# Talking-heads attention with a squared-ReLU FFN: output products that wait for their own quarter of w_out, output evictions ranked last

## The chip, the cores and the metric

The kernel runs on one core of a Trainium2 chip. The metric is the device time of one execution in microseconds, the median of the runs taken. The chip's engines are named as in the profile: PE (TensorE, the matrix engine), DVE (VectorE), ACT (ScalarE), POOL (GpSimd) and SP (SyncE, which issues transfers here). PEld is TensorE's loading of weights, which runs beside its products.

## The reference

Attention over 8 batches, 12 heads, 448 positions and 64 values per head, in which the heads are mixed before and after the softmax, then an FFN with a squared ReLU on all 3584 tokens.

```python
scores = scale * np.matmul(q, k.transpose(0, 1, 3, 2))
scores = np.einsum('bhij,hg->bgij', scores, w_pre)
attn = softmax(scores)                       # over the last axis
attn = np.einsum('bhij,hg->bgij', attn, w_post)
x = np.matmul(attn, v)                       # as (3584, 768)
h = np.maximum(x @ w_in, 0.0)                # w_in (768, 2048)
out = h * h @ w_out                          # w_out (2048, 768)
```

## The kernel before

**The attention.** A batch is cut into 45 chunks of about 10 query rows times 12 heads, 120 of the 128 partitions. For a chunk, TensorE mixes the scores of the heads (lines 901, 907 and, for two chunks at once, 847), VectorE takes the minimum (line 912; the signs are turned), ScalarE the exponential with its sums (line 915), VectorE the reciprocal of the sums (line 922, once for two chunks), GpSimd scales the weights of the second mixing with it (`wq`, line 925), and TensorE forms the mixed attention transposed, four products per chunk (line 932). VectorE or ScalarE copies it to `atb` (the helper `copy`, lines 534 and 536). Scores come from line 741 into `snat` and are laid out anew into the tiles `sch` by transfers that SP issues (`relayout`, line 772). The product with v is line 978. Lines 741 (from batch 1 and for three of four blocks), 847 and 978 run on 64-wide parts of the array, the others on all of it.

**The FFN.** Tokens go in units of 128 or 256 columns of `xt` (`unit`, line 1020). A unit has hidden blocks (line 1037, six products for each 128 of the 2048 hidden values), their ReLU (lines 1051 and 1055) and square (line 1058), and then output blocks: for each 128 tokens two halves of the 768 output columns (0 to 383 and 384 to 767), 16 products each over the hidden values, entered in pairs (`OSTEP = 2`, line 1076). The last 128 tokens have three blocks instead of two. That makes 57 output blocks. Each is copied to `osb` (line 1091) and stored from there (line 1100).

**w_out.** It is loaded in four transfers (`load_w2`, line 1184), each 8 of the 16 hidden groups times one half of the columns: quarters 0 and 1 are the first and second 1024 hidden values of columns 0 to 383, quarters 2 and 3 those of the other columns. They are entered at the chunks of `W2_AT` (14, 17, 20 and 23 of batch 0). The first pair of every output block waits for all four, so the later pairs' own wait adds nothing.

**What sets the order.** All instructions are entered into a planner (`Planner`, line 129) with their dependencies, an estimated duration and a priority, the smaller the earlier; for attention it is the chunk's number with a small offset. The planner goes through time and gives each engine the ready instruction with the smallest priority; that order is then written into the engines' queues, which run it strictly in order. Where an operation has two possible engines, the first that is free takes it. FFN products have priorities of a million and more, so they fill TensorE when attention has nothing ready. The copies of output blocks have priority 0, and so come ahead of nearly all attention work. `AHEAD` is by how many chunks the transfers of `relayout` and the scores rank ahead of the chunk that needs them. An FFN block holds one of eight PSUM banks until it is copied out, and the FFN may hold two at a time (`MOST`). Where TensorE would have nothing up to 130 us of planned time, the planner puts in a matmul on zeros (`stand`, line 1301, the tile `still`), if the array has lately been little used.

Of the kernel before, what the change touches and what calls it, by code (L numbers as in the profile page):

```python
# [19 lines left out]
ACT = mybir.ActivationFunctionType  # L20
# [20 lines left out]
PIECE = NPAIR // 2  # L41
NE = 6
NSCH = 14
AHEAD = 7.0
FIFO = 50
IDLE_NS, IDLE_COLS, IDLE_FROM, IDLE_END, IDLE_LOW = 112, 256, 1300, 130000, 0.62
SPELL, PHASE, DROP, RISE = 3413, 1700, 0.4, 0.8
# [9 lines left out]
OSTEP = 2  # L57
# [28 lines left out]
SOON = 0  # L86
# [42 lines left out]
class Planner:  # L129
# [8 lines left out]
    def add(self, eng, ns, pri, fn, deps=(), lat=60, bank=None, frees=None, mode=0):  # L138
        op = Op(eng if isinstance(eng, dict) else {eng: ns}, lat, pri, fn, list(deps), bank, frees, mode)
        self.ops.append(op)  # L140
        return op
# [199 lines left out]
def kernel(  # L341
# [190 lines left out]
    def copy(eng, out_, in_):  # L532
        if eng == "DVE":
            nc.vector.tensor_copy(out=out_, in_=in_)  # L534
        else:
            nc.scalar.copy(out=out_, in_=in_)  # L536
# [4 lines left out]
    add = pl.add  # L541
    FILL = 1e6
    slots = {}
# [12 lines left out]
    def keep(key, fn):  # L556
        def go(*got):
            for key_, slot in zip(key if isinstance(key, list) else [key], got):
                slots[key_] = slot
            fn(*got)  # L560
        return go
# [10 lines left out]
    m_op, max_op, exp_op, rc_op, wq_op, at_op, ac_op = {}, {}, {}, {}, {}, {}, {}  # L572
    av_op, xc_op = {}, {}
    h_op, sq_op, o_op, st_op = {}, {}, {}, {}
# [137 lines left out]
    def place_of(b, c):  # L712
        return b * NCHUNK + (ORDER0.index(c) if b == 0 else c)
# [4 lines left out]
    direct, prep_op = [], []  # L718

    def is_direct(b, c):  # L720
        return b == 0 and C0[1] <= c <= C0[2]
# [5 lines left out]
    def score(b, r, group):  # L727
# [50 lines left out]
    def relayout(b, c):  # L778
# [6 lines left out]
        deps = list(scopy[b, r]) + (list(scopy[b, r - 1]) if r == 1 and cc == 0 else [])  # L785
        pri = n - AHEAD
        if r == 2 and cc == 0:
# [15 lines left out]
        else:  # L803
            o = cc - 1
            if b >= PAIR_FROM:
                pri = n - o % (2 * PAIRS) + 0.1 * (o % (2 * PAIRS)) - AHEAD
            o, step = (2 * CI * (o // 2) + o % 2, 2) if b >= PAIR_FROM else (o, CPR)
# [207 lines left out]
    def units_of(pair):  # L1015
        return UNITS if pair else UNITS0
# [3 lines left out]
    def unit(pair, ui):  # L1020
        a, z = units_of(pair)[ui]
        w = z - a
        nf = 512 // w
        ix = len(units)
        units.append((pair, ui))
        h2_ = h2[ix % 2]
        fill = FILL + 100 * ix
        xdeps = [op for t0, t1, op in xc_op[pair] if t0 < z and t1 > a]
        old_o = o_op.get(ix - 2, [])
        h_op[pair, a], sq_op[ix], o_op[ix] = [], [], []  # L1030
        prev = None
        for f0 in range(0, FT, nf):
            key = ("f", ix, "h", f0)
            for j in range(nf):
                def mms(slot, f0=f0, j=j):
                    for c2 in range(NPAIR):
                        nc.tensor.matmul(  # L1037
                            slot[:, j * w:(j + 1) * w], lhsT=w1[c2][:, (f0 + j) * 128:(f0 + j + 1) * 128],
                            rhs=xt[:, c2, a:z], start=(c2 == 0), stop=(c2 == NPAIR - 1),
                        )  # L1040
                if j == 0:
                    prev = add("PE", w * 2.55, fill + f0, keep(key, mms), xdeps + w1_in + [prev], lat=0, bank=key)
                else:
                    prev = add("PE", w * 2.55, 0, lambda key=key, mms=mms: mms(slots[key]), [prev], lat=0)
                h_op[pair, a].append(prev)
            end = add("WAIT%s" % str(key), 0, 0, lambda: None, [prev], lat=200)
            gi = len(hr_log)

            def relu(eng, key=key, gi=gi):
                if eng == "DVE":  # L1050
                    nc.vector.tensor_scalar(  # L1051
                        out=hr[gi % 2][:, :], in0=slots[key][:, :], scalar1=0.0, scalar2=0.0, op0=ALU.max, op1=ALU.add,
                    )
                else:
                    nc.scalar.activation(out=hr[gi % 2][:, :], in_=slots[key][:, :], func=ACT.Relu)

            def square(gi=gi, f0=f0):
                nc.gpsimd.tensor_tensor(  # L1058
                    out=h2_[:, f0:f0 + nf, 0:w],
                    in0=hr[gi % 2][:, :].rearrange("p (f c) -> p f c", f=nf),  # L1060
                    in1=hr[gi % 2][:, :].rearrange("p (f c) -> p f c", f=nf), op=ALU.mult,
                )

            rl = add({"ACT": 500, "DVE": 590}, 0, 0, relu, [end, hr_log[gi - 2] if gi >= 2 else None], lat=100, frees=key)
            sq = add("POOL", 1020, FILL, square, [rl] + old_o, lat=70)
            hr_log.append(sq)
            sq_op[ix].append(sq)
        for mt in range(w // 128):
            whole = not (z == W2B and mt == 1 and pair == B // 2 - 1)
            cuts = [0, 384, DMODEL] if whole else [0, 384, 640, DMODEL]  # L1070
            for nt, (c0, c1) in enumerate(zip(cuts, cuts[1:])):
                key = ("f", ix, "o", mt, nt)
                for f0 in range(0, FT, OSTEP):
                    def mms(slot, f0=f0, mt=mt, c0=c0, c1=c1):
                        for ft in range(f0, f0 + OSTEP):
                            nc.tensor.matmul(  # L1076
                                slot[:, 0:c1 - c0], lhsT=h2_[:, ft, mt * 128:(mt + 1) * 128],
                                rhs=w2[:, ft, c0:c1],
                                start=(ft == 0), stop=(ft == FT - 1),
                            )  # L1080
                    if f0 == 0:
                        prev = add("PE", (12 + (c1 - c0) * 5 // 3) * OSTEP / 4, fill + 20 + 4 * mt + 2 * nt, keep(key, mms),
                                   [prev] + sq_op[ix][0:max(1, OSTEP // nf)] + w2_in[0:1 if ix < SOON else 4], lat=0, bank=key)
                    else:
                        prev = add("PE", (12 + (c1 - c0) * 5 // 3) * OSTEP / 4, FILL, lambda key=key, mms=mms: mms(slots[key]), [prev, w2_in[f0 // 4]] + sq_op[ix][0:(f0 + OSTEP + nf - 1) // nf], lat=0)
                    o_op[ix].append(prev)
                end = add("WAIT%s" % str(key), 0, 0, lambda: None, [prev], lat=200)
                si = ix_store[0]

                def evac(eng, key=key, si=si, c0=c0, c1=c1):  # L1090
                    copy(eng, osb[si % 2][:, c0:c1], slots[key][:, 0:c1 - c0])

                ev = add({"DVE": 80 + (c1 - c0) * 25 // 24, "ACT": 165 + (c1 - c0) * 5 // 7}, 0, 0, evac, [end, st_op.get(si - 2)] + ([m_op[n_] for n_ in direct] if si < 2 else []), lat=100, frees=key)
                evs = evs + [ev] if nt == 1 and whole else [ev]
                if nt == 1 or not whole:
                    done = []
                    for rows, dst, o in pieces(pair, a + mt * 128, None if whole else (c0, c1)):
                        side_ = not whole and rows <= CI
                        def store(dst=dst, o=o, rows=rows, si=si, e0=0 if whole else c0, e1=DMODEL if whole else c1, eng=nc.scalar if side_ else nc.gpsimd if whole else nc.sync):
                            eng.dma_start(out=dst, in_=osb[si % 2][o:o + rows, e0:e1])  # L1100
                        done.append(add("ACT" if side_ else "POOL" if whole else "SP", 510 if rows <= CI else 830 if whole else 930, FILL, store, evs))
                    for op in done:
                        op.store = whole
                    st_op[si] = pl.moved("LOAD" if whole else "DMA", 64, 16, 16, 0, done, 700)
            if whole:
                ix_store[0] += 1
# [70 lines left out]
    w2_in = [add("W2", 0, 0, lambda: None, lat=0) for i in range(4)]  # L1177
# [32 lines left out]
    def first_batch():  # L1210
# [35 lines left out]
        for gs in ONE:  # L1246
            av(0, 1, gs, P_ROWS, XB)
        unit(0, 2)

    def next_batch(b):  # L1250
# [91 lines left out]
```

## Time and profile before

| | |
|---|---|
| time before, median of 3 runs | 571.62 us (571.61 to 571.78) |
| profiled execution | 571.9 us, span 570.1 us |
| granted TensorE clock | 0.999 |
| PE, DVE, ACT, POOL busy | 561.1, 500.8, 446.4, 363.0 us |
| instructions at lines 1037, 1076, 932, 1301 on PE | 1632, 912, 1440, 50 |

The span goes from the first to the last instruction; the time of an execution also holds what lies around it. Busy time is the time in which at least one instruction of the engine ran. In the views, a row `start, duration, engine, line, operation, out<-in, xN` merges N instructions that follow each other, and `[idle before <-releaser]` tells how long the engine stood before it and what ended that. Products overlap in the engine, so the duration of a merged row reaches beyond the next row's start; differences of starts tell how long the engine was taken.

### The profile page before, as it was taken

Reading aid. Unit: us, or ns where it says so; the run is one execution under the profiler, and the core shown is the slowest. Engines: PE = TensorE matmul, PEld = TensorE weight load, DVE = VectorE, ACT = ScalarE, POOL = GpSimd, SP = SyncE. Lnnn points to the kernel's source line nnn. Section 1 sums busy time; section 2 is a strip of 40 time slices with the busy share of each in tenths; the row PEclk is TensorE's granted clock in tenths of the full one; section 3 lists DMA queues with packets and bytes.
Section 4 is the critical chain, followed back from the end, with each engine's and each line's share of the span. In section 5 each row is a group of like instructions: output and inputs, shape, how many; then the busy total and the mean of one; then the engine's idle time right before and its main releaser. Section 6 shows DMA issues by size and latency. Waiting matters only on the chain.

```text
span 570.1 us, 17924 instructions
## 1 busy us (share of the span) xinstructions
PE 561.1 (98%) x6340; PEld 398.5 (70%) x6340; DVE 500.8 (88%) x1109; ACT 446.4 (78%) x1186; POOL 363.0 (64%) x677
## 2 busy tenths in 40 slices
PE   8999999999999999999999999999999999999997
PEld 5667765776677767677667677767667677767785
DVE  7999999999999899989888899998899998998542
ACT  5789988788788888888887888987888878888400
POOL 8667346776677448857578456957569554736451
PEclk9999999999999999999999999999999999999999
DMA  9999859974896739964797739975399656542011
GB/s 136 210 177 223 162 122 184 189 146 111 154 208 120 166 101 178 189 149 113 125 213 122 166 101 160 195 163 138 65 208 171 143 139 113 119 103 79 1 56 55
DMA packets 129949, 80.85 MB, mean 142 GB/s; under 512 B 59274, under 2 KB 126588, under 8 KB 129860
## 3 DMA queue, kind: packets, MB, share of 16 engines
q1 hardware_dynamic: 80756, 46.29, 37.0%
q0 software_dynamic: 49104, 33.43, 36.2%
q8 instruction: 49, 0.80, 0.6%
q14 instruction: 40, 0.33, 0.2%
HBM read 45.61 MB, written 11.01 MB: 99 GB/s over the span
## 4 chain that ended last, share of the span: by engine, by line
PE 90%; DVE 6%; POOL 1%; DMA 1%; issue 1%; ACT 0%; DVEq 0%; POOLq 0%; ACTq 0%
PE bank L1076 27%; PE bank L1037 25%; PE bank L932 13%; PE bank L741 7%; PE bank L978 7%; PE bank L847 5%; PE bank L901 3%; PE bank L907 2%; DVE mn L912 1%; DVE snat L534 1%; DMA sch<-snat 1%; DVE atb L534 1%; PE bank L1301 1%; DVE hr L1051 1%; DVE osb L890 1%
## 5 line engine op out<-in xcount | busy, mean ns | idle before, releaser
L915 ACT ACTIVATE es<-bank,mn 124x448 bf16<-124x448 f32 (+1 forms) x360 | 228.1, 642 | 42.9 <-DVE mn L912 35.8
L912 DVE TENSOR_REDUCE mn<-bank 124x1 f32<-124x448 f32 (+1 forms) x360 | 209.4, 613 | 3.9 <-PE bank L847 3.4
L1076 PE MATMUL bank<-w,h 128*128 128x384 bf16 (+2 forms) x912 | 177.3, 323 | 0.2
L1037 PE MATMUL bank<-xt,w 128*128 128x256 bf16 (+1 forms) x1632 | 164.1, 254 | 0.6 <-DVE hr L1051 0.3
L1037 PEld LDWEIGHTS <-w 128*128 128x128 bf16 x1632 | 132.8, 98 | 25.8 <-issue 12.2
L925 POOL TENSOR_SCALAR wq<-wback_two,rc 124x120 bf16<-124x120 f32 x252 | 88.8, 362 | 86.3 <-DVE rc L922 60.2
L1058 POOL TENSOR_TENSOR h<-hr 128x512 bf16<-128x512 f32 x112 | 115.7, 1037 | 33.1 <-DVE hr L1051 15.1
L932 PEld LDWEIGHTS <-es 124*112 124x112 bf16 (+2 forms) x1440 | 108.0, 129 | 32.5 <-issue 8.8
L534 DVE CAST atb<-bank 112x480 bf16<-112x480 f32 (+3 forms) x196 | 119.1, 617 | 10.6 <-PE bank L932 9.6
L932 PE MATMUL bank<-wq,es 124*112 124x120 bf16 (+2 forms) x1440 | 120.2, 217 | 2.0 <-POOL wq L925 1.5
L1076 PEld LDWEIGHTS <-h 128*128 128x128 bf16 x912 | 80.2, 98 | 55.0 <-issue 16.1
L536 ACT CAST atb<-bank 112x480 bf16<-112x480 f32 (+3 forms) x187 | 98.2, 539 | 16.1 <-PE bank L932 14.5
L536 ACT CAST snat<-bank 128x448 bf16<-128x448 f32 x168 | 84.6, 543 | 11.4 <-PE bank L741 10.6
L534 DVE CAST snat<-bank 128x448 bf16<-128x448 f32 x150 | 89.8, 614 | 0.8 <-PE bank L741 0.3
L1051 DVE TENSOR_SCALAR hr<-bank 128x512 f32<-128x512 f32 x82 | 56.6, 690 | 21.1 <-PE bank L1037 15.7
L915 ACT ACTIVATION_READ_ACCUMULATOR es<-bank,mn 124x1 f32 (+1 forms) x360 | 75.0, 208 | 0.0
L925 POOL TENSOR_SCALAR wq<-wback,rc 124x120 bf16<-124x120 f32 (+1 forms) x94 | 33.6, 365 | 39.3 <-DVE rc L922 26.1
L741 PE MATMUL bank<-kt,qz 64*64 64x448 bf16 (+1 forms) x528 | 44.6, 361 | 0.1
L847 PE MATMUL bank<-sch,wmix 64*64 64x448 bf16 x504 | 42.7, 363 | 0.0
L978 PE MATMUL bank<-atb,vs 112*64 112x192 bf16 (+3 forms) x864 | 40.4, 250 | 0.2 <-DVE atb L534 0.2
L978 PEld LDWEIGHTS <-vs 112*64 112x64 bf16 x864 | 36.5, 110 | 5.0 <-issue 4.5
L1100 POOL DMA_DIRECT2D out_dram<-osb x33 | 19.9, 604 | 29.9 <-DVE osb L534 16.4
(80 smaller groups left out, 397.7 us busy)
## 6 DMA issues: line engine op xcount, KB each, us to landing
sch<-snat SPq DMA_DIRECT2D x318, 105.0 KB
out_dram<-osb POOLq DMA_DIRECT2D x21, 384.0 KB, 3.8
vs<-in_v_dram POOLq DMA_DIRECT2D x16, 336.0 KB, 7.8
ks<-in_k_dram POOLq DMA_DIRECT2D x14, 336.0 KB, 8.0
qs<-in_q_dram POOLq DMA_DIRECT2D x14, 288.0 KB, 8.4
w<-in_moe_w_in_dram POOLq DMA_DIRECT2D x6, 512.0 KB, 13.0
w<-in_moe_w_out_dram POOLq DMA_DIRECT2D x4, 768.0 KB, 21.1
out_dram<-osb POOLq DMA_DIRECT2D x8, 192.0 KB, 7.5
```

The lines of the kernel that those rows point to most:

```text
L534: nc.vector.tensor_copy(out=out_, in_=in_)
L536: nc.scalar.copy(out=out_, in_=in_)
L741: nc.tensor.matmul(slot[m0:m1, 0:S], lhsT=lhsT[:, m0:m1], rhs=kt[i][half, :, at_, :], start=True, stop=True,)
L847: nc.tensor.matmul(got[i + x][o0:o1, 0:S], lhsT=w[k0:k1, c0:c0 + o1 - o0], rhs=srcs[i + y][k0:k1, :], start=True, stop=True,)
L912: nc.vector.tensor_reduce(out=mn[i][0:rows, :], in_=slots[mk][0:rows, 0:S], axis=AX.X, op=ALU.min)
L915: nc.scalar.activation(out=es[i][0:rows, 0:S], in_=slots[mk][0:rows, 0:S], func=ACT.Exp, scale=-1.0, bias=mn[i][0:rows, 0:1], accum_out=sm ...
L925: nc.gpsimd.tensor_scalar(out=wq[i][0:rows, :, 0:ns], in0=back[0:rows, :, 0:ns], scalar1=rc[i // 2][0:rows, i % 2:i % 2 + 1], scalar2=1.0, ...
L932: nc.tensor.matmul(slot[0:P_KEYS, jb * H * ns:(jb + 1) * H * ns], lhsT=es[i][0:rows, jb * P_KEYS:(jb + 1) * P_KEYS], rhs=wq[i][0:rows, :, ...
L978: nc.tensor.matmul(v_[64 * hh:64 * hh + 64, i, 0:x1 - x0], lhsT=vs[:, 2 * c2 + hh, jb, :], rhs=atb[half][:, jb, 2 * c2 + hh, x0:x1], start ...
L1037: nc.tensor.matmul(slot[:, j * w:(j + 1) * w], lhsT=w1[c2][:, (f0 + j) * 128:(f0 + j + 1) * 128], rhs=xt[:, c2, a:z], start=(c2 == 0), sto ...
L1058: nc.gpsimd.tensor_tensor(out=h2_[:, f0:f0 + nf, 0:w], in0=hr[gi % 2][:, :].rearrange("p (f c) -> p f c", f=nf), in1=hr[gi % 2][:, :].rear ...
L1076: nc.tensor.matmul(slot[:, 0:c1 - c0], lhsT=h2_[:, ft, mt * 128:(mt + 1) * 128], rhs=w2[:, ft, c0:c1], start=(ft == 0), stop=(ft == FT - 1),)
```

## The change

It has three parts. Each pair of output products waits for the one quarter that it reads (column half `c0 // 384`, hidden half `f0 // 8`); the first pair of a block no longer waits for all four loads. The copies of output blocks get priority 100000, behind all attention work on VectorE and ScalarE but ahead of nothing else that matters there. `AHEAD` goes from 7.0 to 7.4.

```diff
-AHEAD = 7.0
+AHEAD = 7.4
...
                     if f0 == 0:
                         prev = add("PE", (12 + (c1 - c0) * 5 // 3) * OSTEP / 4, fill + 20 + 4 * mt + 2 * nt, keep(key, mms),
-                                   [prev] + sq_op[ix][0:max(1, OSTEP // nf)] + w2_in[0:1 if ix < SOON else 4], lat=0, bank=key)
+                                   [prev, w2_in[2 * (c0 // 384)]] + sq_op[ix][0:max(1, OSTEP // nf)], lat=0, bank=key)
                     else:
-                        prev = add("PE", ..., [prev, w2_in[f0 // 4]] + sq_op[ix][0:(f0 + OSTEP + nf - 1) // nf], lat=0)
+                        prev = add("PE", ..., [prev, w2_in[2 * (c0 // 384) + f0 // 8]] + sq_op[ix][0:(f0 + OSTEP + nf - 1) // nf], lat=0)
...
-                ev = add({"DVE": 80 + (c1 - c0) * 25 // 24, "ACT": 165 + (c1 - c0) * 5 // 7}, 0, 0, evac, [end, st_op.get(si - 2)] + ..., lat=100, frees=key)
+                ev = add({"DVE": 80 + (c1 - c0) * 25 // 24, "ACT": 165 + (c1 - c0) * 5 // 7}, 0, 100000.0, evac, [end, st_op.get(si - 2)] + ..., lat=100, frees=key)
```

More of the change, by code (lines that the diff above doesn't have):

```diff
@@ L1082, in unit @@
                         prev = add("PE", (12 + (c1 - c0) * 5 // 3) * OSTEP / 4, fill + 20 + 4 * mt + 2 * nt, keep(key, mms),
-                                   [prev] + sq_op[ix][0:max(1, OSTEP // nf)] + w2_in[0:1 if ix < SOON else 4], lat=0, bank=key)
+                                   [prev, w2_in[2 * (c0 // 384)]] + sq_op[ix][0:max(1, OSTEP // nf)], lat=0, bank=key)
                     else:
-                        prev = add("PE", (12 + (c1 - c0) * 5 // 3) * OSTEP / 4, FILL, lambda key=key, mms=mms: mms(slots[key]), [prev, w2_in[f0 // 4]] + sq_op[ix][0:(f0 + OSTEP + nf - 1) // nf], lat=0)
+                        prev = add("PE", (12 + (c1 - c0) * 5 // 3) * OSTEP / 4, FILL, lambda key=key, mms=mms: mms(slots[key]), [prev, w2_in[2 * (c0 // 384) + f0 // 8]] + sq_op[ix][0:(f0 + OSTEP + nf - 1) // nf], lat=0)
                     o_op[ix].append(prev)
@@ L1091, in evac @@
                     copy(eng, osb[si % 2][:, c0:c1], slots[key][:, 0:c1 - c0])
-                ev = add({"DVE": 80 + (c1 - c0) * 25 // 24, "ACT": 165 + (c1 - c0) * 5 // 7}, 0, 0, evac, [end, st_op.get(si - 2)] + ([m_op[n_] for n_ in direct] if si < 2 else []), lat=100, frees=key)
+                ev = add({"DVE": 80 + (c1 - c0) * 25 // 24, "ACT": 165 + (c1 - c0) * 5 // 7}, 0, 100000.0, evac, [end, st_op.get(si - 2)] + ([m_op[n_] for n_ in direct] if si < 2 else []), lat=100, frees=key)
                 evs = evs + [ev] if nt == 1 and whole else [ev]
```

## The prediction

> **What bounds the kernel now.** I read the page first: the busy shares, the slices, the chain.
>
> ```profile
> span 570.1 us, 17924 instructions
> PE 561.1 (98%) x6340; PEld 398.5 (70%) x6340; DVE 500.8 (88%) x1109; ACT 446.4 (78%) x1186; POOL 363.0 (64%) x677
> ...
> PE   8999999999999999999999999999999999999997
> PEclk9999999999999999999999999999999999999999
> ...
> PE 90%; DVE 6%; POOL 1%; DMA 1%; issue 1%; ACT 0%; DVEq 0%; POOLq 0%; ACTq 0%
> ```
>
> TensorE (PE) is busy for 98% of the span and carries 90% of the chain that ended last. So the time is the work in TensorE's queue plus the few microseconds in which it stands still. VectorE at 88% matters only where it makes TensorE stand. To see where that is, I asked for the busy time in windows of 10 us.
>
> ```profile
> core 0: us, PE busy (x) PEld busy (x) DVE busy (x) ACT busy (x) POOL busy (x), PEclk, DMA share, GB/s
> 0.00:10.00 10.00, 8.94 (x75) 5.62 (x77) 6.26 (x25) 3.62 (x6) 8.55 (x17) 1.00 0.96 114
> 10.00:20.00 10.00, 8.91 (x90) 5.54 (x85) 9.66 (x31) 8.31 (x20) 8.44 (x17) 1.00 1.36 200
> ...
> 60.00:70.00 10.00, 9.34 (x154) 7.28 (x149) 9.71 (x24) 9.35 (x28) 3.10 (x7) 1.00 0.77 153
> 70.00:80.00 10.00, 9.29 (x122) 7.00 (x120) 9.46 (x20) 8.48 (x23) 5.16 (x11) 1.00 0.55 120
> 80.00:90.00 10.00, 9.57 (x128) 5.67 (x127) 9.91 (x23) 9.44 (x28) 7.44 (x15) 1.00 0.69 133
> ...
> 560.00:570.00 10.00, 6.96 (x59) 4.92 (x57) 1.83 (x4) 0.00 (x0) 0.59 (x1) 0.95 0.21 79
> sum 570.00, PE 561.10 PEld 398.51 DVE 500.77 ACT 446.41 POOL 363.00; mean PE 9.84 PEld 6.99 DVE 8.79 ACT 7.83 POOL 6.37
> ```
>
> Of the 8.9 us that TensorE is idle (570.0 - 561.1), 2.15 lie in the first 20 us and 3.04 in the last window, after the last product. The change reaches neither. 1.80 lie between 60 and 90 us; the other 1.9 are scattered. But "busy" hides one thing: the planner writes matmuls on zeros (line 1301, the tile `still`) into TensorE's queue where it expects nothing to do. The timeline of TensorE around 80 us shows them.
>
> ```profile
> 58.78 0.38 PE L932 MATMUL bank<-wq,es 124*112 124x120 bf16 x4
> ...
> 65.30 0.42 PE L932 MATMUL bank<-wq,es 124*112 124x120 bf16 x4
> ...
> 74.94 0.63 PE L932 MATMUL bank<-wq,es 124*112 124x120 bf16 x8
> ...
> 76.18 0.80 PE L932 MATMUL bank<-wq,es 124*112 124x120 bf16 x8
> 76.81 0.73 PE L901 MATMUL bank<-sch,wmix 124*128 124x448 bf16 x3
> 77.38 1.91 PE L1301 MATMUL bank<-still 128*128 128x256 bf16 x16
> 80.41 0.37 PE L932 MATMUL bank<-wq,es 124*112 124x120 bf16 x4 [1.12 <-POOL wq L925]
> ...
> 82.85 0.49 PE L1076 MATMUL bank<-w,h 128*128 128x384 bf16 x2
> ```
>
> From 77.38 to 80.41 TensorE does nothing useful: 16 fillers in 1.91 us, then 1.12 us of waiting for `wq` of the next chunk. That is one hole of 3.0 us. The hidden activations of unit 0 were there, but its output products (line 1076) stand only behind it, the first at 82.85, because their opening pair was made to wait for all four loads of w_out. The issue and landing of those four, asked one by one:
>
> ```profile
> L1186 POOL DMA_DIRECT2D w<-in_moe_w_out_dram x1: 928/928/928, 40.3 to 40.3; - x1
> ...
> DMA to landing us min/median/max: 16.4/16.4/16.4
> ...
> L1186 POOL DMA_DIRECT2D w<-in_moe_w_out_dram x1: 922/922/922, 43.3 to 43.3; - x1
> ...
> DMA to landing us min/median/max: 20.2/20.2/20.2
> ...
> L1186 POOL DMA_DIRECT2D w<-in_moe_w_out_dram x1: 939/939/939, 48.3 to 48.3; - x1
> ...
> DMA to landing us min/median/max: 22.0/22.0/22.0
> ...
> L1186 POOL DMA_DIRECT2D w<-in_moe_w_out_dram x1: 927/927/927, 51.0 to 51.0; - x1
> ...
> DMA to landing us min/median/max: 25.1/25.1/25.1
> ```
>
> The quarters land at 56.7, 63.5, 70.3 and 76.1 us. The last is there before the hole opens at 77.38: the hole was left in the order because the planner expected the quarters later or had nothing else ready, not because the chip still waited.
>
> **Part 1, the wait for the quarter.** The built order of the changed kernel (counts only, no times) has 6323 products against 6340. The difference is fillers alone, 33 against 50. The first 28 stand as before; the 16 of the hole are gone. The output products of unit 0 now begin behind the 29th chunk's products of line 932, which is the row of 58.78. They read quarter 0 there, 2.1 us or more after its landing at 56.7. Quarter 1 is first read behind the 34th chunk (65.30, landed 63.5), quarter 2 behind the 39th (inside the row of 74.94, landed 70.3). Quarter 3 is read behind the 42nd and behind 24 products of line 1037, so after 77, landed 76.1. No quarter should stop TensorE. POOL still issues the four loads behind the same chunks' `wq`, so their landing should not move by much. Between the 42nd chunk and the 43rd the new order has 24 products of line 1037 and, around them, six of line 1076, where the fillers were.
>
> The price: 17 fillers at 1.91 / 16 = 0.12 us are 2.0 us. The wait of 1.12 us ends later in the queue and has real work ahead of it: 1.1 us. What that work would have cost later is saved, because TensorE is full afterwards.
>
> Is there enough work to fill with? In the new order 64 output products of older units stand behind the last attention products, 40 before. So the stock never runs out, and work taken forward leaves no hole behind.
>
> **Part 2, AHEAD and the rank of evictions.** Both reshuffle the whole order; the instructions stay. `AHEAD` 7.0 to 7.4 lets SP's relayouts and TensorE's scores rank 0.4 chunk earlier, which moves them past each other but adds no transfer. The evictions of line 1093 go behind all attention work on VectorE and ScalarE: 35 and 22 of them instead of 30 and 27. The relu moves the other way (76 and 36 instead of 82 and 30).
>
> ```profile
> L534 DVE COPY osb<-bank x30: 292/548/558, 89.7 to 567.0; 128x384 f32<-128x384 f32 x28, 128x256 f32<-128x256 f32 x1, 128x128 f32<-128x128 f32 x1
> ...
> L1051 DVE TENSOR_SCALAR hr<-bank 128x512 f32<-128x512 f32 x82 | 56.6, 690 | 21.1 <-PE bank L1037 15.7
> L912 DVE TENSOR_REDUCE mn<-bank 124x1 f32<-124x448 f32 (+1 forms) x360 | 209.4, 613 | 3.9 <-PE bank L847 3.4
> ```
>
> VectorE gets 5 x 0.55 - 6 x 0.69 = -1.4 us of work. It lies beside TensorE's and I put it at nothing; if VectorE were the bound in some stage it would be worth at most that 1.4.
>
> What a reshuffle does to TensorE's own time is the number of turns between products on the whole array and products on 64-wide parts (lines 741, 847, 978). Two pairs of rows price a turn: output products followed by a full product, and by one on parts.
>
> ```profile
> 89.00 1.15 PE L1076 MATMUL bank<-w,h 128*128 128x384 bf16 x6
> 90.08 0.38 PE L847 MATMUL bank<-sch,wmix 64*64 64x448 bf16 x4
> ...
> 95.71 0.82 PE L1076 MATMUL bank<-w,h 128*128 128x384 bf16 x4
> 96.37 0.38 PE L932 MATMUL bank<-wq,es 124*112 124x120 bf16 x4
> ```
>
> Four products before a full one take 96.37 - 95.71 = 0.66 us, 0.165 each. Six before a turn take 1.08 where 6 x 0.165 = 0.99: a turn costs 0.09 us. The order before has 324 turns, the changed one 311. 13 fewer are 1.2 us. The Trainium skill, TensorEngine Tiling (Array Packing), section Key Properties, says that a change of tiling mode drains the engine. It gives no price; the trace agrees in kind with its 0.09 us.
>
> The three edits built alone say which does what: the quarter alone leaves 34 fillers and 309 turns, the rank alone 50 and 308, `AHEAD` alone 42 and 316. The turns are luck of the order; the fillers belong to the first edit.
>
> **The sum.** 2.0 + 1.1 + 1.2 = 4.3 us. The profiled execution took 571.9 us (its span 570.1, 1.8 outside it): 567.6 after. The median of the runs shown is 571.62, 0.3 lower: 567.3 us.
>
> Bounds. If three small holes near 60 us (part of the 0.66 idle in that window) and about half of the scattered 1.9 also go, it is 1.6 better: 565.7, and I take 565.4. New holes of the same kind can open, and a turn's 1.2 us is the least firm term.
>
> **Rivals.**
>
> *The hole only moves.* What ends the hole is the chunk's own chain (minimum, exponential, reciprocal, `wq`). If that chain has no slack after 80 us either, TensorE meets it a little further on with its stock already spent there. For it: VectorE is busy 9.46 and 9.91 of 10 us in the two windows. Against it: from 90 us on windows are full, and the last rows of the tail have stock. Then only the turns are left: 571.6 - 1.2 = 570.4.
>
> *A quarter lands late (slower).* The first output pair now stands in TensorE's queue at about 59 us, with everything else behind it. If load 0 took 25.1 us as load 3 did, it would land at 65.4 and TensorE would stand for 6.4 us: 567.3 + 6.4 = 573.7. It turns into slower once the load takes 7.5 us longer than its 16.4 (2.1 of margin and 5.4 of gain and threshold). Against it: nothing is put ahead of that load on its queue, and load 3 is slow because the other loads are ahead of it.
>
> The trace shows what a cold array costs:
>
> ```profile
> 1.06 3.81 PE bank L1301 x17
> ```
>
> The same filler takes 3.81 / 17 = 0.22 us at the start and 0.12 at 77 us, although the granted clock reads 1.00 in both windows. So a long stand would also make the products after it dear. The Trainium skill, TensorE: Matmul & The Clock Gate, section "What's actually happening", halves the clock after an idle window of about 3.4 us, for at least a window of that length. By it such a stand would cost about 1.7 us more, as an estimate; no stand that long is in this trace.
>
> *Evictions come too late (slower).* The FFN has two banks, and a block whose eviction waits holds one. In both built orders the closest case has one block of hidden products between a block's last product and the next use of a bank.
>
> ```profile
> 54.39 1.45 PE bank L1037 x24
> ```
>
> That is 1.45 us of cover. An eviction of 0.55 behind one minimum of 0.61 fits (1.16); behind two (1.77) TensorE loses 0.3 us. There are 57 such blocks. It becomes slower than before by more than the threshold from 18 of them on (5.4 / 0.3); at 25 it is 567.3 + 7.5 = 574.8. Against it: few blocks are at that closest distance, and ScalarE has 22% free.
>
> **How the numbers follow.** A measurement of this kernel can tell about 0.2%, 1.1 us, from no change. The forecast of 567.3 has 0.76 with its own spread of 565.4 to 569.5; the hole that moves 0.12, on both sides of the 570.5 edge (a third of it faster); a late quarter 0.05; late evictions 0.07. So faster 0.80, same 0.08, slower 0.12. The range runs from 565.4 to 570.9, over the moved hole's 570.4 and half a microsecond more; outside lie the two slow rivals and little else.
>
> **What would show it.** In the changed profile: 33 instructions at line 1301, none after 40 us; a first instruction at line 1076 near 59 us; windows 60 to 90 with TensorE at about 10 each; no wait of TensorE for w_out in the list of waits; the last product some 4 us before 567, with the same 3 us of idle TensorE behind it. A wait at line 1076 for the load, or windows after 100 us below 9.8, would show one of the slow rivals. TensorE idle again around 80 to 90 us would show the moved hole.

## The result: 1.9 us faster, less than half of what was forecast

The changed kernel takes 569.74 us (median of 6 runs, 568.32 to 570.19) against 571.6 us before on the same chip: a ratio of 0.9964 with a 95% interval of 0.9951 to 0.9977. The forecast was 567.3. The direction is right, the size is not. The profiled execution took 569.92 us.

The page of the changed kernel:

```profile
span 567.8 us, 17932 instructions
...
PE 559.7 (99%) x6323; PEld 396.5 (70%) x6323; DVE 496.8 (87%) x1108; ACT 447.9 (79%) x1187; POOL 363.7 (64%) x677
...
PE 86%; DVE 5%; ACT 3%; issue 2%; POOL 2%; DMA 1%; DVEq 0%; ACTq 0%; POOLq 0%
```

TensorE's busy time fell by 1.4 us only (561.1 to 559.7), and its share of the chain from 90% to 86%, while ScalarE's rose from 0 to 3% and GpSimd's from 1 to 2%: waits on them now stand in it. First, what was foreseen. The fillers of the changed kernel:

```profile
L1301 PE MATMUL bank<-still x33: 267/421/422, 1.1 to 39.1; 128*128 128x256 bf16 x28, 64*128 64x256 bf16 x5
```

Its loads of w_out, and their time from issue to landing:

```profile
L1186 POOL DMA_DIRECT2D w<-in_moe_w_out_dram x4: 922/936/947, 39.8 to 52.2; - x4
...
DMA to landing us min/median/max: 16.0/20.6/24.2
```

Its timeline of TensorE where the first output products stand, and where the hole was:

```profile
60.27 0.49 PE L1076 MATMUL bank<-w,h 128*128 128x384 bf16 x2
...
78.97 1.50 PE L1037 MATMUL bank<-xt,w 128*128 128x128 bf16 x24
80.30 0.49 PE L1076 MATMUL bank<-w,h 128*128 128x384 bf16 x2
80.95 0.71 PE L932 MATMUL bank<-wq,es 124*112 124x120 bf16 x8 [0.16 <-POOL wq L925]
```

33 fillers, the last at 39.1; the first output pair at 60.27, without a wait; no load that stops TensorE; and work where the fillers had stood, with 0.16 us of waiting for `wq` in the place of 1.12. The windows of the changed kernel show that the early gain is there, and that something is given back later:

```profile
60.00:70.00 10.00, 9.95 (x131) 6.91 (x131) 9.89 (x24) 9.84 (x28) 3.12 (x10) 1.00 0.78 153
70.00:80.00 10.00, 9.91 (x147) 7.78 (x144) 9.58 (x20) 8.23 (x22) 4.53 (x8) 1.00 0.52 118
80.00:90.00 10.00, 9.84 (x133) 6.36 (x131) 9.00 (x22) 9.15 (x24) 7.56 (x14) 1.00 0.64 117
...
180.00:190.00 10.00, 9.42 (x93) 6.09 (x93) 9.75 (x22) 8.48 (x24) 6.45 (x16) 1.00 0.71 156
```

From 60 to 90 us TensorE is idle for 0.30 us, where it was 1.80. But the window from 180 to 190 has lost 0.58. The list of TensorE's waits in the changed kernel (us in total, times, longest) has new ones, among them:

```profile
PE bank L901 <- DVE atb L534: 0.6, 1, 0.6
...
PE bank L932 <- ACT es L915: 0.3, 1, 0.3
```

The timeline of the changed kernel shows the first of them, in that window:

```profile
183.62 0.67 PE L932 MATMUL bank<-wq,es 124*112 124x120 bf16 x8
184.87 0.35 PE L901 MATMUL bank<-sch,wmix 124*128 124x448 bf16 x1 [0.58 <-DVE atb L534]
```

**How kernels are compared below.** No view adds up what is lost in gaps too small to be listed, so I worked out one figure. A step is the difference of the starts of two products that follow each other on TensorE; its price is the median step of the same kind of pair in the trace before (0.162 us after a 384-column product, 0.109 after a 256-column one, 0.09 more at a turn). *Lateness* is the sum of steps minus prices. Some 6.2 us of it in each trace is only the coarse price of line 741. The *lead* is how much sooner a kernel would end than the one before, if neither had any lateness behind the products of the 60th chunk (at about 100 us). Lead and lateness come from the one profiled execution of each kernel. Before, 252 FFN products are done by then and the lateness behind it is 11.0 us. In the changed kernel 352 are done: the lead is 5.1 us, more than the 4.3 forecast. But the lateness behind it is 13.8, so 2.8 us are given back, and 2.3 are left in the span (570.1 to 567.8). 2.3 of the 2.8 arise between chunks 60 and 150, from 104 to 232 us.

### The profile page after: what moved, and what is told of

Read it like the earlier page. It is cut to its first block, busy times and chain, and to the rows that moved or that the text cites. A ratio compares the mean times of both kernels' runs of the same rounds, so it can differ in the third digit from the quotient of the medians.

```text
span 567.8 us, 17932 instructions
## 1 busy us (share of the span) xinstructions
PE 559.7 (99%) x6323; PEld 396.5 (70%) x6323; DVE 496.8 (87%) x1108; ACT 447.9 (79%) x1187; POOL 363.7 (64%) x677
## 3 DMA queue, kind: packets, MB, share of 16 engines
HBM read 45.61 MB, written 11.01 MB: 100 GB/s over the span
## 4 chain that ended last, share of the span: by engine, by line
PE 86%; DVE 5%; ACT 3%; issue 2%; POOL 2%; DMA 1%; DVEq 0%; ACTq 0%; POOLq 0%
PE bank L1076 25%; PE bank L1037 24%; PE bank L932 13%; PE bank L978 6%; PE bank L741 6%; PE bank L847 5%; PE bank L901 3%; DVE mn L912 2%; ACT es L915 2%; PE bank L907 1%; DMA sch<-snat 1%; PE bank L1301 1%; DVE atb L534 1%; PE bank L596 1%; POOL wq L925 1%
## 5 line engine op out<-in xcount | busy, mean ns | idle before, releaser
L1076 PE MATMUL bank<-w,h 128*128 128x384 bf16 (+2 forms) x912 | 180.2, 324 | 0.2 <-DVE hr L1051 0.2
L536 ACT CAST atb<-bank 112x480 bf16<-112x480 f32 (+3 forms) x187 | 99.2, 542 | 17.8 <-PE bank L932 16.6
L1051 DVE TENSOR_SCALAR hr<-bank 128x512 f32<-128x512 f32 x76 | 52.2, 688 | 19.4 <-PE bank L1037 16.5
L741 PE MATMUL bank<-kt,qz 64*64 64x448 bf16 (+1 forms) x528 | 45.8, 361 | 0.7 <-ACT qz L536 0.6
L1100 POOL DMA_DIRECT2D out_dram<-osb x33 | 19.8, 600 | 35.5 <-DVE osb L534 18.1
```

The source lines that it names most:

```text
L741: nc.tensor.matmul(slot[m0:m1, 0:S], lhsT=lhsT[:, m0:m1], rhs=kt[i][half, :, at_, :], start=True, stop=True,)
L1076: nc.tensor.matmul(slot[:, 0:c1 - c0], lhsT=h2_[:, ft, mt * 128:(mt + 1) * 128], rhs=w2[:, ft, c0:c1], start=(ft == 0), stop=(ft == FT - 1),)
```

## The experiments

### One edit at a time

Each kernel has some of the three edits (the quarter: both dependency lines; the rank: priority 100000; `AHEAD` 7.4).

```diff
# quarter alone; with the rank; with AHEAD
-  [prev] + sq_op[ix][...] + w2_in[0:1 if ix < SOON else 4]
+  [prev, w2_in[2 * (c0 // 384)]] + sq_op[ix][...]
# rank, AHEAD
-  0, 0, evac          -AHEAD = 7.0
+  0, 100000.0, evac   +AHEAD = 7.4
```

> The wait for the own quarter alone; rank of evictions and AHEAD as before. The built order has 34 fillers and 309 turns of the array (before: 50 and 324). Sum as in the prediction: fillers 16 x 0.12 = 1.9, the wait in the hole 1.1, 15 turns x 0.09 = 1.4, together 4.4: 567.2 us from 571.6. Theory 'the rank costs' (late evictions eat 2 us of the gain in the changed kernel): 567.2 here. Theory 'AHEAD costs' (7.4 eats the 2 us): 567.2 here. Theory 'luck of the order' (every reshuffle has its own small waits of TensorE, of some 2 us either way): 565.5 to 569.5, with the number of TensorE steps that are over 0.2 us late going with the distance from 567.2.

> Quarter and rank of evictions, AHEAD stays at 7.0. 34 fillers, 309 turns: by the sum 4.4 us less, 567.2. Theory 'the rank costs': 569.2 (the 2 us are lost here too). Theory 'AHEAD costs': 567.2. Theory 'luck of the order': 565.5 to 569.5, and not tied to what the quarter alone gives.

> Quarter and AHEAD 7.4, evictions ranked as before. 33 fillers but 331 turns: by the sum 2.0 + 1.1 - 7 x 0.09 = 2.5 us less, 569.1. Theory 'the rank costs': 569.1. Theory 'AHEAD costs': 571.1. Theory 'luck of the order': 567.5 to 571.

> Rank and AHEAD 7.4 without the quarter: all output blocks wait for all of w_out again. 42 fillers, 322 turns: by the sum 8 x 0.12 + 2 x 0.09 = 1.1 us less if the hole of 3 us stays with its remaining fillers, 570.5. Theory 'the rank costs' or 'AHEAD costs': 572.5. Theory 'luck of the order': 569 to 572.5. In the trace the hole should stand near 77 to 80 us with some 8 fillers and a wait for wq behind them.

> The rank of evictions alone. 50 fillers, 308 turns: the hole stays, by the sum 16 turns x 0.09 = 1.4 us less, 570.2. Theory 'a reshuffled order has its own small waits': 570.2 plus 2 to 9 us, as the four other partial orders had behind 100 us (13 to 21 us of lateness against 11.0), so 572 to 579; likeliest 575.

> AHEAD 7.4 alone. 42 fillers, 316 turns: by the sum 0.9 + 0.7 = 1.6 us less, 570.0. Theory 'a reshuffled order has its own small waits': 572 to 579, likeliest 575. If AHEAD as such is good (relayouts earlier, fewer waits of TensorE for sch): below 570 and fewer waits for sch than in the kernel before.

> The changed kernel with AHEAD 7.35 instead of 7.4, which reshuffles the order once more: 33 fillers as in the changed kernel, 319 turns instead of 311. Sum of the prediction: 2.0 + 1.1 + 5 x 0.09 = 3.6 us below 571.6, 568.0. Theory 'AHEAD costs' as a trend: as the changed kernel, 569.7 plus 0.7 for the turns, 570.4. Theory 'luck of the order': anything from 568 to 575, as the three partial versions gave; a distance of over 2 us from the changed kernel at the same fillers speaks for it.

> The changed kernel once more, for a second profile and its spread. 569.7 us, between 568.3 and 570.2. If its small waits behind 100 us (some 14 us of lateness against prices of TensorE's steps, 11 in the kernel before) are a matter of this order, they stand at the same places again: L901 at 184.9 (0.6 us) and L847 at 161 among them. If they are a matter of the run, they stand elsewhere.

| order | us, median (before 571.6) | lead at the 60th chunk | lateness behind it |
|---|---|---|---|
| before | 571.6 | 0 | 11.0 |
| rank | 572.89 (572.33 to 574.15) | 0.7 | 12.9 |
| AHEAD | 574.38 (572.36 to 576.34) | -0.1 | 13.3 |
| rank and AHEAD | 575.05 (573.57 to 577.15) | -1.0 | 13.2 |
| quarter | 572.65 (570.95 to 573.7) | 6.2 | 16.6 |
| quarter and rank | 575.29 (574.42 to 577.81) | 6.5 | 20.8 |
| quarter and AHEAD | 573.91 (572.86 to 575.48) | 2.9 | 17.5 |
| all three | 569.74 (568.32 to 570.19) | 5.1 | 13.8 |
| all three, again | 569.74 (569.18 to 570.31) | 5.2 | 14.3 |
| all three, AHEAD 7.35 | 576.62 (574.85 to 577.84) | 4.5 | 19.8 |

The profiled execution is not always near the median (571.21 us for the quarter, 575.48 for the quarter with `AHEAD`).

Every one of these orders but the changed kernel came out slower than the kernel before, and the first four slower than every theory that was written down for them, "luck of the order" with its 2 us either way included.

Three things follow. The quarter gives the lead: every order that has it gains 2.9 to 6.5 us by the 60th chunk, none of the others more than 0.7. Every reshuffled order pays more behind: those without the quarter 1.9 to 2.3 us over the order before, the changed kernel 2.8, its neighbours with the quarter 5.6 to 9.8. And neither the rank nor `AHEAD` has an effect of its own: the rank costs 1.3 us on the kernel before (571.6 to 572.89) and 2.6 on the quarter, and gains 4.2 on the quarter with `AHEAD`; `AHEAD` costs 2.8 alone and gains 5.6 on the quarter with the rank. A step from 7.4 to 7.35 costs 6.9. Part of these distances is the granted clock (last section). That all three edits together beat the kernel before is the luck of this one order. The change run again gives the same time, and its largest wait, 0.6 us at line 901, stands there again.

The two columns depend on how a step is priced. With the bursts of line 741 priced by fours, entries move by up to 1.8 us: the leads are then 3.8 to 6.1 us with the quarter and 0.7 to 1.9 without it, and the lateness over that of the order before is 3.0 to 4.1 us without the quarter, 3.2 in the changed kernel, and 5.4 to 9.3 in its neighbours. So the changed kernel pays about what the reshuffles without the quarter pay.

Where do these orders lose it? In part in waits for the transfers of `relayout`. The list of TensorE's waits from 100 to 530 us in the rank with `AHEAD`, and then in the quarter with `AHEAD`:

```profile
PE bank L901 <- DMA sch<-snat: 2.2, 1, 2.2
...
PE bank L847 <- DMA sch<-snat: 2.3, 2, 1.9
```

The first wait, at 121 us, is as long as the whole 2.2 us that its order loses; the two waits of the second, near 158 us, are a third of the 6.5 of theirs. The rank alone has one of 0.9, `AHEAD` alone one of 0.5, the order before and the first profile of the changed kernel none that the list shows.

### Is the hole worth its 3 us?

Both kernels have the order before, rearranged by hand. In the first the 16 fillers of 77 us go, and the 16 products of the first output block take their place; in the second the 16 fillers just go.

```diff
-        for op, args in pl.run():
+        sched = pl.run()
+        gaps = [i for i, (op, _) in enumerate(sched) if op.fn is stand][-16:]
+        # first: the eight pairs o_op[0][0:8] at gaps[0], two banks exchanged
+        # second: nothing in their place
```

> The order of the kernel before, kept by hand: the 16 fillers of the hole at 77 us are taken out, and the 16 products of the first output block stand in their place, in a bank that is free there (two banks change names behind it). Nothing else of the order changes. Theory 'the hole is worth its length' (prediction): 16 x 0.163 = 2.6 us of real work move into 3.0 us of hole, nothing is lost elsewhere, 571.6 - 2.6 = 569.0 (568.6 to 569.5). Theory 'the hole only moves' (the chunks' own chain is the bound behind 80 us as well): 571 to 571.6, with a new wait of TensorE for wq or es before 100 us. Theory 'luck of the order' says nothing against 569.0, since the order stays: it is the test that a gain without a reshuffle comes out whole.

> The order of the kernel before with the 16 fillers of the hole left out and nothing in their place. The chunks' chain ends the hole, so TensorE should stand from 77.4 to about 80.4. If fillers cost no time of their own: 571.6, with a wait of 3.0 us for wq. If the clock falls for the stand: the products behind it run at half speed for about 3.4 us, 1.7 us more, 573.3, and the granted clock in 80 to 90 us reads about 0.83. If the fillers delay the chain itself (they take no bank or port that it needs, so I do not expect it): below 571.

Filled: 571.64 us (570.89 to 573.39), a ratio of 0.9998 with 0.9985 to 1.001, so nothing of the 2.6 us is gained that can be told from the noise. Without fillers: 572.82 us (571.96 to 573.88), 1.2 slower. The timeline of the filled one:

```profile
77.27 2.76 PE L1076 MATMUL bank<-w,h 128*128 128x384 bf16 x16 [0.64 <-DVE atb L534]
79.87 0.38 PE L932 MATMUL bank<-wq,es 124*112 124x120 bf16 x4
80.47 0.57 PE L741 MATMUL bank<-kt,qz 64*64 64x448 bf16 x8 [0.22 <-ACT es L915]
...
81.61 0.35 PE L901 MATMUL bank<-sch,wmix 124*128 124x448 bf16 x1 [0.23 <-DVE snat L534]
```

`wq` is no longer late, but the block itself starts 0.64 us late, and the products behind it now wait for the exponential (`es`) and for `snat`: lateness from 60 to 100 us rises from 2.4 to 5.6, all that was gained. In this stretch the hole only moves. The timeline of the kernel without fillers:

```profile
79.87 0.56 PE L932 MATMUL bank<-wq,es 124*112 124x120 bf16 x4 [2.87 <-POOL wq L925]
```

And its windows:

```profile
70.00:80.00 10.00, 7.13 (x101) 5.11 (x99) 9.67 (x21) 8.47 (x23) 5.15 (x10) 0.97 0.55 125
80.00:90.00 10.00, 10.00 (x112) 6.54 (x112) 7.60 (x18) 7.30 (x22) 4.97 (x11) 0.69 0.60 119
```

The wait lasts nearly as long as the fillers and the old wait together (3.0), and after it the granted clock is 0.69; these are the runs that are 1.2 us slower. So the fillers stood beside a wait and cost nothing; counting them as work removed was wrong for this place.

### What a microsecond of TensorE is worth later

```diff
+        extra = None
         for op, args in pl.run():
+            if extra is None and op.at > 118000 and op.bank and op.bank[0][0] == "f" and op.bank[0][2] == "h":
+                extra = op
+                for _ in range(24):
+                    stand(args[0], 0)
             op.fn(*args)
```

> The kernel before, its order untouched, with 24 more matmuls on zeros ahead of the first hidden block planned after 118 us, in that block's own bank: 24 x 0.11 = 2.6 us of useless work where TensorE's windows are full. Theory 'from 100 us on TensorE is the bound and every microsecond counts once': 571.6 + 2.6 = 574.2 (573.8 to 574.6), and the lateness of the later steps stays at 11 us. If attention's chain has the slack of the two engines to share (as between 77 and 90 us, where 3 us filled with work brought nothing): 571.6 to 572.6. Together with the filled hole it says which of the two stretches pays for work moved ahead.

574.32 us (574.2 to 574.69) beside 571.64: 2.68 more, and the lateness behind the 60th chunk is that of the order before. In this order, at the one place tried (122 us), each microsecond on TensorE counts once. That supports, for the stretches where TensorE is full, that FFN products taken forward save their time later, as long as nothing new stands still.

### Mending the two largest new waits of the changed kernel

```diff
+        # (in words) two pairs of output products ahead of the mix that waits at 184.9,
+        # six hidden products ahead of the chunk that waits at 490.8
```

> The changed kernel with two places of its order mended by hand and nothing else moved: at 184.9 us two pairs of output products go ahead of the mix that waits 0.6 us for a bank, and at 490.8 us six hidden products go ahead of a chunk whose exponential is 0.3 us late. Theory 'the lost part of the gain is these small waits, one by one': 0.75 + 0.39 = 1.1 us less than the changed kernel, 568.6 (568.2 to 569.1), with both waits gone from the trace and the rest of the lateness as it was. If the waits only move to the next product: 569.7.

570.45 us (568.82 to 571.9), no gain. The timeline of this kernel:

```profile
184.81 0.81 PE L1076 MATMUL bank<-w,h 128*128 128x384 bf16 x4 [0.21 <-ACT es L915]
...
491.34 0.81 PE L1037 MATMUL bank<-xt,w 128*128 128x256 bf16 x6 [0.64 <-DVE hr L1051]
```

The first wait has shrunk from 0.58 to 0.21 us. The second has only another name: the bank that the block needs was not free yet (`hr`, the ReLU of line 1051), 0.64 us. Lateness stays at 14.0.

### Is it VectorE's limit?

VectorE is busy for 9.0 to 9.9 of 10 us in the windows shown, and I had come to think that the orders with the quarter run against that limit. Four orders, unchanged, with a shorter minimum:

```diff
-  nc.vector.tensor_reduce(..., in_=slots[mk][0:rows, 0:S], ...)
+  nc.vector.tensor_reduce(..., in_=slots[mk][0:rows, 0:S // 2], ...)
```

> The kernel before, its order unchanged on every engine, with the minimum of line 912 taken over 224 of the 448 columns (the shift of the exponential is then the extreme of half the row: that part of the computation is left out). 360 instructions on VectorE get shorter by about 0.25 us each, 90 us in all, so VectorE is no longer near its limit anywhere. Theory (the lateness behind 100 us comes from VectorE running at its limit): lateness falls from 11.0 to about 7, of which 6.2 is the coarse price of line 741; about 567.5 us. Rival (it comes from the length of the chunk's chain through ScalarE, GpSimd and the transfers, in which the minimum is one link): lateness falls by 1 to 2 us; about 570.

> The changed kernel with the same short minimum and its own order unchanged. Theory (VectorE's limit): lateness falls from 13.8 to the same 7, so the lead of 5.1 us that it has at the 60th chunk survives: about 562.5 us, 5 us below the kernel before with the short minimum. Rival (the chain, or gaps that the order has whatever VectorE does): the two stay 2 us apart, about 568.

> The quarter and the rank without AHEAD (20.8 us of lateness, 575.29 us) with the same short minimum and its own order unchanged. Theory (VectorE's limit): lateness falls to about 7 and, as its priced work is the least of all orders, it becomes the fastest: about 561 us. Rival: it stays some 4 us slower than the kernel before with the short minimum, about 574.

> The quarter alone (16.6 us of lateness, 572.65 us) with the same short minimum and its own order unchanged. Theory (VectorE's limit): about 561.5 us, 6 below the kernel before with the short minimum. Rival: 1 us above that kernel, about 571.

The minimum in the kernel before, made shorter:

```profile
L912 DVE TENSOR_REDUCE mn<-bank x360: 368/380/393, 17.0 to 526.2; 124x1 f32<-124x224 f32 x168, 120x1 f32<-120x224 f32 x7, 100x1 f32<-100x224 f32 x5
```

The busy shares on that kernel's page:

```profile
PE 560.1 (99%) x6340; PEld 398.0 (70%) x6340; DVE 430.0 (76%) x1109; ACT 448.6 (79%) x1186; POOL 364.8 (64%) x677
```

| order | us | lateness behind the 60th chunk, full and short minimum |
|---|---|---|
| before | 569.33 (568.81 to 569.39) | 11.0, 10.0 |
| all three | 568.7 (567.15 to 570.63) | 13.8, 12.3 |
| quarter and rank | 574.79 (573.38 to 576.34) | 20.8, 19.9 |
| quarter | 570.16 (569.2 to 571.39) | 16.6, 14.7 |

VectorE has 71 us less to do, and the lateness falls by only 1 to 2 us in each, so the orders' distances in lateness stay (the 1.9 us in time between the changed kernel and the one before shrink to 0.6, within the scatter of its runs). In time, too, the orders with the quarter are 6 to 14 us above what the theory gave them. This theory fell. What the worst order still showed was one stretch, 207 to 221 us, with 6.4 us of lateness where it had 7.1.

### The stretch at the batch boundary

There batch 2 ends: its last tokens come to `xt` only with the products of line 978, and a burst of scores (line 741) of the next batch stands in the queue. TensorE's timeline of the quarter with the rank (full minimum):

```profile
206.38 0.49 PE L1076 MATMUL bank<-w,h 128*128 128x384 bf16 x2
206.80 1.11 PE L741 MATMUL bank<-kt,qz 64*64 64x448 bf16 x10
...
211.80 0.79 PE L741 MATMUL bank<-kt,qz 64*64 64x448 bf16 x6 [0.44 <-DVE osb L534]
213.77 0.70 PE L932 MATMUL bank<-wq,es 124*112 124x120 bf16 x8 [1.18 <-POOL wq L925]
...
216.67 3.61 PE L978 MATMUL bank<-atb,vs 112*64 112x256 bf16 x48
...
221.27 0.94 PE L1037 MATMUL bank<-xt,w 128*128 128x256 bf16 x7
```

The windows of 5 us of the same kernel:

```profile
205.00:210.00 5.00, 4.60 (x49) 2.13 (x46) 4.84 (x10) 4.88 (x13) 0.70 (x2) 1.00 0.26 58
210.00:215.00 5.00, 3.06 (x29) 1.64 (x29) 4.31 (x12) 5.00 (x15) 2.24 (x6) 0.99 0.53 144
215.00:220.00 5.00, 4.94 (x58) 4.08 (x57) 4.06 (x9) 3.63 (x11) 2.49 (x6) 0.67 0.54 142
```

Between 206.87 and 221.27 there is no FFN product at all: all tokens delivered so far are used up. TensorE's attention products alone are priced at 7.6 us, but they take 7.1 more, while ScalarE is busy almost without a break from 205 to 215 us (4.88 and 5.00 of 5.00). 0.8 of the 7.1 is line 978 at a lower clock (3.61 us; 2.81 below). The timeline of the kernel before has FFN work left there:

```profile
206.76 2.77 PE L1076 MATMUL bank<-w,h 128*128 128x384 bf16 x16
...
211.37 0.49 PE L1076 MATMUL bank<-w,h 128*128 128x384 bf16 x2
...
212.49 2.81 PE L978 MATMUL bank<-atb,vs 112*64 112x256 bf16 x48
...
217.65 0.82 PE L1076 MATMUL bank<-w,h 128*128 128x384 bf16 x4
...
218.91 1.48 PE L1037 MATMUL bank<-xt,w 128*128 128x256 bf16 x12
```

From the built orders I added up the FFN products that are delivered but not done when the next tokens come near 215 us, at the prices above (an estimate): 1.0 us before, 0.3 in the changed kernel, 0 in the four others with the quarter (`AHEAD` 7.35 among them), 1.9 to 2.6 in the three others without it. The longest stretch without FFN there and its lateness: 4.0 us and 0.3 (before, and the changed kernel), 4.8 and 0.7 (with `AHEAD`), 6.1 and 3.2 (`AHEAD` 7.35), 6.3 and 2.8 (quarter alone), 7.6 and 7.1 (with the rank). So an empty stock need not cost much: with `AHEAD` it costs 0.7, and that order loses most of its time elsewhere. The last two runs put work into that stretch of the worst order, and take it out of the order before:

```diff
# shortened; quarter and rank: five pairs of unit 5's last block later
+        spots = [found["g", "s", 3, 1, 5, 0], found["m", 133], found["a", 130], found["m", 136], found["m", 137]]
+        # o_op[5][11:16], one behind each
# before: six pairs of the same block earlier
+        # o_op[5][10:16] directly behind o_op[5][9]
```

> The order of the quarter with the rank (575.29 us). In it the FFN has no product left between 206.8 and 220.6 us: all tokens that attention has delivered are used up, the next are written to xt only at 220.3, and TensorE stands while ScalarE is busy without a break. Five pairs of output products (1.6 us) that ran just before, at 201.8 to 206.4, are put between the attention products of 206.8 to 209.5; nothing else moves, and the total work of TensorE is the same. Theory (TensorE stands because the stock of FFN work is spent): the lateness between 195 and 240 us falls by 0.8 to 1.6 of its 7 us, and the time by as much, to about 574.1. Rival (the chain of the chunks holds TensorE there whatever lies between): the stands move to 202 to 206 and the time stays at 575.3.

> The order before, in which the same stretch has FFN products among the attention products until the new tokens come at 218.9 us. Six pairs of output products (1.9 us) that stand there between 210.3 and 218.4 us are brought forward to 209.7, behind their block's first two pairs, so that the stretch runs dry; no attention product can get earlier than before by it, and none more than 1.9 us later, so the loss lies between 0 and 1.9 us. Theory (stock spent): TensorE stands between 212 and 219 us, lateness there up by 0.6 to 1.9; about 572.8. Rival (where the FFN work stands does not matter): 571.6.

Fed: 575.9 us (574.68 to 577.3) beside 575.29, no gain; here the rival came true. Its lateness there is 7.2 instead of 7.1, of which 2 to 3 us now lie from 202 to 208. Drained: 573.39 us (573.26 to 574.94) beside 571.57, 1.8 slower, nearly all of the 1.9 us that was put ahead of the chain. The timeline of the drained order:

```profile
206.43 4.71 PE L1076 MATMUL bank<-w,h 128*128 128x384 bf16 x28
...
213.70 2.81 PE L978 MATMUL bank<-atb,vs 112*64 112x256 bf16 x48
...
219.48 0.38 PE L847 MATMUL bank<-sch,wmix 64*64 64x448 bf16 x4 [0.18 <-DVE atb L534]
220.01 1.47 PE L1037 MATMUL bank<-xt,w 128*128 128x256 bf16 x12
```

Its windows:

```profile
210.00:215.00 5.00, 4.83 (x56) 3.44 (x55) 3.61 (x8) 3.40 (x10) 0.70 (x2) 1.00 0.54 129
215.00:220.00 5.00, 4.57 (x68) 2.97 (x65) 5.00 (x12) 4.28 (x11) 3.32 (x6) 1.00 0.55 109
```

The same work in another place, and the hidden products start at 220.01 instead of 218.91; the stretch has 7.0 us of attention and 2.2 of lateness, where it had 4.0 and 0.3. Together the two runs say: around the batch boundary the pace is set by the chunks' chain through VectorE, ScalarE and GpSimd. FFN products between its steps cost nothing there, and an order that has spent them stands, wherever its last ones are put. What such an order won by spending them early is paid back. Which of the three engines sets the pace was not tested; the short minimum left 6.4 of the 7.1 us, which speaks against VectorE, and ScalarE is the one without free time.

## Why the prediction was right in direction and wrong in size

**Part 1, the loads and the fillers: foreseen.** The quarters landed between 55.8 and 76.4 us and stopped nothing; 17 fillers went, 16 of them at the place named; the 60 to 90 us windows are at 9.84 to 9.95. The late quarter did not happen, and no wait for `osb` stands in the list of TensorE's waits, so late evictions are not seen. Two windows after 100 us are below 9.8 all the same (9.42 from 180, 9.68 from 490 us): the sign that was meant for the slow rivals came here from waits for `atb` and `es`, which no rival had named.

**Part 1, the price: right as a sum, wrong as a mechanism.** I added 2.0 us of fillers and 1.1 of waiting as work taken off the path. Filling that hole alone gives 0.0 (between 0.6 lost and 0.9 gained), since the next links of the chain are just as late. The changed kernel's lead comes with 100 more FFN products done by the 60th chunk, in gaps from 60 us on; no run shows which of these gaps gives how much. With the 13 turns the lead is 5.1 us, beside 4.3 forecast. The rival "the hole only moves" was right for the stretch from 77 to 100 us.

**Part 2, the reshuffle at turns and else nothing: the step that failed.** The turns came as counted. But I let the new order have no other cost, with half a sentence on "new holes". It has 2.8 us more lateness behind the 60th chunk, which takes the 5.1 us of lead down to the 2.3 by which the span fell, and neighbouring orders have 1.9 to 9.8 more. That term should have been in the sum with a spread of several microseconds: the nine orders of the first table lie between 569.74 and 576.62 us.

**"So the stock never runs out": wrong.** I looked at the tail, where there is plenty. At the batch boundary the order before has 1.0 us of FFN work left, and a change that does 100 FFN products sooner must come through there. The changed kernel does so with 0.3 us left and almost no stand; three of its neighbours pay 2.8 to 7.1.

**What stays open.** The changed kernel's own 2.8 us are many waits of 0.1 to 0.8 us, most from 104 to 232 us, where it has less FFN work in stock than the order before. Too little stock would explain them, but that was shown only for its neighbours at the batch boundary and for the drained order before, and the three orders without the quarter, with more stock there than the order before, lose 1.9 to 2.3 us as well. Mending the two largest waits by hand gained nothing; no version was found that beats the changed kernel.

The last product ends 2.3 us sooner than before, not the 4 that were written down, with the same 3 us behind it.

## What to carry to other kernels

Where a planner writes the order, a changed dependency is a new order: price it with the spread of its neighbours (here 7 us), not with the instructions that it removes, and build two or three neighbours before believing an edit. Filling a hole of one engine pays, by the runs here, only if the filling is taken from a place where that engine is the bound and the next link of the chain is not as late; put the same work into the hole by hand to see. Work that fills gaps is a stock: look for its lowest level along the whole span, above all where new input is delivered, not only at the end.

## What the hardware did that was not expected

**The clock falls after a short stand.** TensorE stood for 2.87 us without fillers, and the next window was granted 0.69; in finer windows the granted clock is 0.50 from 79.4 to 86.2 us and 1.00 from there. In the quarter with `AHEAD` TensorE was busy for 2.68 us from 155 to 160, the next 5 us were granted 0.72, and 12 products of line 1037 took 2.64 us instead of 1.48. In the quarter with the rank it was busy for 3.06 of 5 us, in pieces, and the next 5 us had 0.67: 48 products of line 978 took 3.61 us where they take 2.81 at full clock. The drained order, which stood for 0.17 and 0.43 us in such windows, kept 1.00. The Trainium skill, TensorE: Matmul & The Clock Gate, section "What's actually happening", gives the drop after an idle window of about 3.4 us; the traces agree in kind, but here stands below 3 us in one piece were enough. The clock is also part of the distances between orders: of the eleven runs of the quarter alone the four with a granted clock of 0.999 or more took 570.95 to 571.71 us, and six of the seven with 0.996 or 0.997 took 572.65 to 573.7. So the 1.1 us by which its median lies above the kernel before goes with the clock.

**The lateness of the order before repeats.** The order before has 11.02, 11.01 and 11.00 us of it from 100 us on in three kernels (itself, hole filled, no fillers), though the three differ at 77 us. The reshuffled orders repeat less well: the two profiles of the changed kernel have 13.8 and 14.3, the second with one more wait of 0.6 us for a relayout (line 847), and the runs of the quarter with `AHEAD` lie between 572.86 and 575.48. So a difference of half a microsecond between two such orders can't be read from single traces.
